# Attention in a three-part kernel: scores of a pair of heads in four steps, transposes in eight, and an order that counts changes of TensorE's tiling

## The chip, the cores and the metric

The kernel runs on one core of a Trainium2 chip. The metric is device time in microseconds (us) of one execution; a lower number is better. Three executions of the kernel before took 2150.86, 2153.95 and 2156.48 us, so the median is 2153.95 us. A further execution was recorded by the hardware profiler; everything read from the trace comes from that one.

## What is computed

Three parts follow each other: an attention with a memory term, a dense mixture of experts (all eight experts on every token, weighted by a normalised table P), and a routed mixture in which a token goes to one expert or to none. The change is in the first part only. Its reference, shortened:

```
B, H, S, D = 4, 8, 576, 64
scores = where(causal, -1e9, q @ k.T / sqrt(D))
a = exp(scores - scores.max(-1));  a /= a.sum(-1)
q_p = where(q > 0, q, exp(q) - 1) + 1
mem_out = (q_p @ M_prev) / (q_p @ z_prev)
g = 1 / (1 + exp(-beta))
out = g * mem_out + (1 - g) * (a @ v)
x = out.transpose(0, 2, 1, 3).reshape(B * S, H * D)      # 2304 x 512, input of the experts
```

All numbers are float32.

## The kernel before

The 32 heads are worked off as 16 pairs. The 576 query rows of a head are cut into five query tiles: tile 0 has 64 rows, tiles 1 to 4 have 128, and because of the causal mask they look at 64, 192, 320, 448 and 576 keys. For a pair the steps are these.

- **scores** (L211, TensorE, matmul on L219): the two heads of a pair have D = 64 each, so head 0 lies on partitions 0 to 63 and head 1 on 64 to 127. Their matmuls use 64 rows of the array each. This is the first of three tilings of the array; the trace shows it as `64*128`. There are six chunks a pair: one for each of the tiles 0 to 3 and two of 288 keys for tile 4. Each chunk takes one PSUM bank per head out of a ring of four banks (two chunks).
- **rowmax** (L224, VectorE): mask, copy into an SBUF tile `pe`, and the row's maximum. There are six `pe` tiles, and ten are needed for a pair.
- **exp** (L239, ScalarE, with the row sums), **mem** (L245, GpSimd: puts the scaled memory query in front of the 64 first columns of `pe`).
- **transposes** (L263, TensorE, L268): blocks of 128 by 128 of `pe` into a PSUM tile `t`, with the whole array, the second tiling (`128*128`). A head has chunks of 1, 2, 3, 4, 4 and 1 blocks; each takes one of two `t` banks. **evac** (L270, ScalarE or VectorE) copies it to SBUF, `pt`.
- **pv** (L285, TensorE, L294): five steps that multiply with the values; the outputs of the two heads lie on 64 columns of the array each, the third tiling (`128*64`).
- **norm** (VectorE) and **norm_rows** (GpSimd, L260) make the row factors; **factors** (L300, TensorE, whole array, L306 and L308, in a `t` bank) turns them, and **finish** (VectorE) multiplies and writes the input `x` of the experts.
- **phi_exp** (ScalarE), **phi** (VectorE), **phi_z** (GpSimd, L199) and **mem_norm** (VectorE) prepare the memory query of a later pair. **logits** (L481, TensorE, 8 columns wide, in a `t` bank) are the gate scores of the experts for the rows of `x` that are done; 13 such steps run inside the attention.

The order of all these steps on each engine is made when the program is built, by a list planner (class `List`, L38). Each step has a length, an urgency, steps that must come before it, and rings of buffers that it takes and gives back. At each moment a free engine takes the ready step with the smallest urgency (L85). The urgency of a step is the pair's number times `PER` plus an entry of the table `AT`. The planner knows nothing of the array's tilings. On the chip each engine then works its list in order, and waits on semaphores where a step isn't ready.

When the last pair is done the experts begin (matmuls on L572); their first weights are requested while the attention still runs.

## Time and profile before

| | us |
|---|---|
| median of three executions | 2153.95 |
| profiled execution, its own time | 2153.33 |
| its span, first to last instruction | 2151.6 |
| attention, from the span's start to the first matmul of the experts | 260.4 |
| TensorE's matmuls busy in the attention | 237.2 |
| VectorE, ScalarE, GpSimd busy in the attention | 171.35, 188.64, 129.50 |
| TensorE busy in the rest, 1891.2 us | 1865.75 |

The busy time of TensorE counts matmuls in flight. The end of a matmul is modelled in the profile, and matmuls overlap; the distance from the start of one group to the start of the next is therefore the better measure of what a group costs. In the trace each float32 matmul of scores and of pv stands as two passes, so a step on two heads reads "x4"; a transpose stands once.

### The profile page before, as it was taken

How to read it: one execution, taken by the hardware profiler on the slowest of the kernel's cores; microseconds unless marked ns; L12 is line 12 of the kernel's file. 1: busy time of each engine (PE TensorE's matmuls, PEld its weight loads, DVE VectorE, ACT ScalarE, POOL GpSimd, SP SyncE). 2: the span in 40 equal slices, each digit the busy share in tenths (PEclk: the TensorE clock that was granted, in tenths of full speed). 3: DMA queues.
4: the chain of work that ended last, by engine and by line, in shares of the span. 5: the costliest groups of instructions: out<-in, count | busy, mean ns of one | idle time of the engine just before them, and what ended most of it. 6: DMA issues, size and time to landing. Idle time of an engine off the chain costs nothing.

```text
span 2151.6 us, 33371 instructions
## 1 busy us (share of the span) xinstructions
PE 2102.9 (98%) x11986; PEld 1771.2 (82%) x11986; DVE 1500.1 (70%) x3182; ACT 804.2 (37%) x1937; POOL 574.6 (27%) x654
## 2 busy tenths in 40 slices
PE   7999899999999999999999999999999999999997
PEld 4455488998899889988888988898899888788886
DVE  5667658777777777777777777777777777434563
ACT  6777632332223223323433322232223223334463
POOL 4445612222222222222312222222222222311121
PEclk9999989999999999999999999999999999899999
DMA  4332211111111111111211211111111111134551
GB/s 113 92 86 74 65 45 40 50 49 41 40 50 50 40 40 50 50 40 55 69 40 49 80 49 40 49 45 45 40 50 50 40 40 64 55 117 150 206 176 50
DMA packets 124800, 138.34 MB, mean 64 GB/s; under 512 B 48202, under 2 KB 83018, under 8 KB 124624
## 3 DMA queue, kind: packets, MB, share of 16 engines
q1 hardware_dynamic: 120704, 126.67, 18.6%
q0 software_dynamic: 3920, 9.44, 1.3%
q8 instruction: 96, 1.57, 0.3%
q14 instruction: 80, 0.66, 0.1%
HBM read 195.86 MB, written 10.75 MB: 96 GB/s over the span
## 4 chain that ended last, share of the span: by engine, by line
PE 89%; DVE 3%; DMA 3%; issue 2%; ACT 1%; POOL 0%; SPq 0%; POOLq 0%; DVEq 0%; ACTq 0%
PE pm L572 32%; PE psy L641 12%; PE psy L643 12%; PE psy L642 12%; PE s L219 3%; PE o L294 3%; PE t L268 3%; DMA out_dram<-o,idx 1%; PE psh L1442 1%; PE psh L1440 1%; PE psh L1441 1%; PE psy L1464 1%; PE psy L1465 1%; PE psy L1466 1%; DMA xg<-out_dram,idx 1%
## 5 line engine op out<-in xcount | busy, mean ns | idle before, releaser
L572 PE MATMUL pm<-xch,w1h 128*128 128x288 f32 (+2 forms) x1792 | 536.5, 299 | 4.2 <-DVE u L585 3.4
L572 PE MATMUL pm<-xch,w1l 128*128 128x288 f32 (+2 forms) x1792 | 531.4, 297 | 2.9 <-DVE w1l L543 2.9
L572 PE MATMUL pm<-xcl,w1h 128*128 128x288 f32 (+2 forms) x1792 | 530.1, 296 | 0.0
L652 DVE SCALAR_TENSOR_TENSOR acc<-psy,pr,acc 128x512 f32<-128x512 f32 x504 | 377.9, 750 | 156.2 <-PE psy L643 145.7
L641 PE MATMUL psy<-w2h,h 128*128 128x512 f32 x1152 | 458.7, 398 | 0.4 <-ACT h L599 0.4
L643 PE MATMUL psy<-w2h,h 128*128 128x512 f32 x1152 | 456.8, 397 | 0.0
L642 PE MATMUL psy<-w2l,h 128*128 128x512 f32 x1152 | 456.3, 396 | 0.0
L585 DVE TENSOR_TENSOR u<-pm,u 128x288 f32<-128x288 f32 (+2 forms) x640 | 290.1, 453 | 121.4 <-PE pm L572 101.3
L572 PEld LDWEIGHTS pm<-xch,w1h 128*128 128x128 f32 x1792 | 339.5, 189 | 10.3 <-DVE u L585 5.9
L572 PEld LDWEIGHTS pm<-xch,w1l 128*128 128x128 f32 x1792 | 339.6, 189 | 3.7 <-DVE w1l L543 3.7
L572 PEld LDWEIGHTS pm<-xcl,w1h 128*128 128x128 f32 x1792 | 339.9, 190 | 2.7
L599 ACT ACTIVATE h<-u 128x288 fp32r<-128x288 f32 (+4 forms) x512 | 182.1, 379 | 361.1 <-DVE u L585 360.9
L537 POOL TENSOR_TENSOR s<-raw 128x256 f32<-128x256 f32 x128 | 95.5, 746 | 819.9 <-issue 800.9
L603 DVE SCALAR_TENSOR_TENSOR h<-u,h 128x288 fp32r<-128x288 f32 (+4 forms) x512 | 258.1, 533 | 69.1 <-ACT h L599 63.1
L609 ACT ACTIVATE u<-pm 128x288 f32<-128x288 f32 (+2 forms) x128 | 51.2, 400 | 682.1 <-PE pm L572 682.1
L643 PEld LDWEIGHTS psy<-w2h,h 128*128 128x128 f32 x1152 | 217.0, 188 | 54.8 <-DVE h L603 1.6
L641 PEld LDWEIGHTS psy<-w2h,h 128*128 128x128 f32 x1152 | 216.8, 188 | 49.5 <-ACT h L599 1.0
L642 PEld LDWEIGHTS psy<-w2l,h 128*128 128x128 f32 x1152 | 216.9, 188 | 49.1
L543 POOL TENSOR_TENSOR w2l<-raw,w2h 128x1024 fp32r<-128x1024 f32 x64 | 154.2, 2410 | 308.5 <-ACT w2h L540 303.6
L268 PEld LDWEIGHTS t<-ident,pe 128*128 128x128 f32 x480 | 54.5, 146 | 64.4 <-issue 25.4
L235 DVE CUSTOM_DVE_ANT_0 pe<-s,mask 128x64 f32<-128x64 f32 (+4 forms) x160 | 65.9, 425 | 49.1 <-PE t L268 38.6
L268 PE MATMUL t<-ident,pe 128*128 128x128 f32 x480 | 85.2, 296 | 12.3 <-ACT pt L283 8.3
(289 smaller groups left out, 2685.9 us busy)
## 6 DMA issues: line engine op xcount, KB each, us to landing
rw<-in_moe_w_dram SPq DMA_DIRECT2D x94, 1024.0 KB
raw<-in_moe_w_dram SPq DMA_DIRECT2D x131, 512.0 KB
qn<-in_qn_dram SPq DMA_DIRECT2D x16, 320.0 KB
vm<-in_vm_dram SPq DMA_DIRECT2D x32, 160.0 KB
q<-in_qT_dram SPq DMA_DIRECT2D x16, 288.0 KB
k<-in_kT_dram SPq DMA_DIRECT2D x16, 288.0 KB
out_dram<-acc SPq DMA_DIRECT2D x18, 256.0 KB
zb<-in_z_prev_dram SPq DMA_DIRECT2D x16, 64.0 KB
```

Source lines behind the costliest of these rows:

```text
L235: nc.vector.tensor_tensor_reduce(s["pe", i][:, 64 + k0:64 + k1], self.raw.pop(("s", n, c)), self.mask[:, m0 + k0:m0 + k1], -0.125, s["nb2" ...
L268: self.nc.tensor.transpose(t[:, kk - k0, :], pe[:, kk * P:(kk + 1) * P], self.ident)
L537: return lambda: nc.gpsimd.tensor_tensor(o, x, y, op)
L543: return lambda: eng.tensor_tensor(o, src, f32(h), ALU.subtract)
L572: nc.tensor.matmul(o, w, x, start=start and k == 0 and i == 0, stop=k == 1 and i == 2, skip_group_check=not start)
L585: nc.vector.tensor_tensor(o, a, b, ALU.add)
L599: nc.scalar.activation(o, src[:, i], AF.Relu)
L603: nc.vector.scalar_tensor_tensor(o, src[:, i], 0.0, f32(hi), ALU.max, ALU.subtract)
L641: nc.tensor.matmul(ps, hh[:, ts], h2[:, f, :], start=f == 0, stop=False)
L642: nc.tensor.matmul(ps, hh[:, ts], l2[:, f, :], start=False, stop=False)
L643: nc.tensor.matmul(ps, hl[:, ts], h2[:, f, :], start=False, stop=f == 1)
L652: nc.vector.scalar_tensor_tensor(a, ps, self.pr[:, j, e:e + 1], a, ALU.mult, ALU.add)
```

## The change

- **Scores in four steps.** `SC` lists for each step the tile, the keys from and to, and the column in the bank. Tiles 1 and 2 (192 + 320 columns) share a bank, tiles 0 and 3 (64 + 448) share one, and tile 4 keeps its two steps of 288. The six pieces of each head stay, and so do the six row maxima.
- **Transposes in eight steps for a pair** in place of twelve: tile 1 of both heads in one bank, tiles 2 and 0 of one head in one bank, the last block of tile 4 of both heads in one bank. The copies out (evac) are as many as before, now up to two from one bank, one after the other.
- **The planner** adds `TURN` to a TensorE step whose tiling differs from the one before it, and `STAY` to its urgency. `PER`, `AT` and the lengths have new values.
- A step that reads a shared bank waits for the whole step that fills it, and a bank comes free when its last reader is done.

The core of the diff:

```
-SC = [(i, k0, k1) for i in range(NQ) for k0, k1 in ([(0, NK[i])] if NK[i] <= 512 else [(0, NK[i] // 2), (NK[i] // 2, NK[i])])]
-TC = [(0, 0, 1), (1, 0, 2), (2, 0, 3), (3, 0, 4), (4, 0, 4), (4, 4, 5)]
+SC = [[(1, 0, 192, 0), (2, 0, 320, 192)], [(0, 0, 64, 0), (3, 0, 448, 64)], [(4, 0, 288, 0)], [(4, 288, 576, 0)]]
+TC = [[(0, 1, 0, 2), (1, 1, 0, 2)], [(0, 2, 0, 3), (0, 0, 0, 1)], [(1, 2, 0, 3), (1, 0, 0, 1)], [(0, 3, 0, 4)], [(1, 3, 0, 4)],
+      [(0, 4, 0, 4)], [(1, 4, 0, 4)], [(0, 4, 4, 5), (1, 4, 4, 5)]]
...
+    TURN, STAY = 0.17, 9.41
...
-                k = min(go, key=lambda k: steps[k][3])
+                turn = {k: e == "PE" and self.mode[k] != mode for k in go}
+                k = min(go, key=lambda k: steps[k][3] + self.STAY * turn[k])
...
-                free[e] = end = now + engines[e]
+                free[e] = end = now + engines[e] + self.TURN * turn[k]
...
-        i, k0, k1 = SC[c]
-        for j in range(2):
-            r = slice(j * 64, j * 64 + 64)
-            o = self.ps_s.tile([P, 512], F32, name="s")[:, :k1 - k0]
-            nc.tensor.matmul(o, q[r, Q0[i]:Q0[i] + P], k[r, k0:k1], start=True, stop=True)
-            self.raw["s", 2 * m + j, c] = o
+        banks = [self.ps_s.tile([P, 512], F32, name="s") for _ in range(2)]
+        for i, k0, k1, a in SC[c]:
+            for j in range(2):
+                r = slice(j * 64, j * 64 + 64)
+                o = banks[j][:, a:a + k1 - k0]
+                nc.tensor.matmul(o, q[r, Q0[i]:Q0[i] + P], k[r, k0:k1], start=True, stop=True)
+                self.raw["s", 2 * m + j, i, k0] = o
...
+    def transposes(self, m, c):
+        t, a = self.ps_t.tile([P, 4, P], F32, name="t"), 0
+        for j, i, k0, k1 in TC[c]:
+            pe = self.st[2 * m + j]["pe", i]
+            self.raw["t", 2 * m + j, i, k0] = t[:, a:a + k1 - k0]
+            for kk in range(k0, k1):
+                self.nc.tensor.transpose(t[:, a, :], pe[:, kk * P:(kk + 1) * P], self.ident)
+                a += 1
...
-    PER = 11.33
+    PER = 12.84
...
```

Three places show what the new order does. The first is TensorE's list in the middle of the attention, before: the transposes of a pair alternate with the next pair's scores (`s` are score banks, `t` transpose banks, `pe` the tiles that are turned; "x4" is four blocks).

```order
L268 MATMUL t_1555<-ident_58,pe_1471 128x128 x4
L219 MATMUL s_1561<-k_1324,q_1323 128x192
L219 MATMUL s_1563<-k_1324,q_1323 128x192
L268 MATMUL t_1578<-ident_58,pe_1490 128x128 x4
L219 MATMUL s_1585<-k_1324,q_1323 128x320
L219 MATMUL s_1587<-k_1324,q_1323 128x320
L268 MATMUL t_1599<-ident_58,pe_1493 128x128 x4
L268 MATMUL t_1605<-ident_58,pe_1490 128x128
L268 MATMUL t_1615<-ident_58,pe_1493 128x128
L219 MATMUL s_1617<-k_1324,q_1323 128x448
L219 MATMUL s_1619<-k_1324,q_1323 128x448
```

The same place after the change:

```order
L229 MATMUL s_1496<-k_1317,q_1316 128x64
L229 MATMUL s_1497<-k_1317,q_1316 128x64
L229 MATMUL s_1496<-k_1317,q_1316 128x448
L229 MATMUL s_1497<-k_1317,q_1316 128x448
L278 MATMUL t_1505<-ident_58,pe_1434 128x128 x4
L278 MATMUL t_1518<-ident_58,pe_1445 128x128 x4
L229 MATMUL s_1540<-k_1317,q_1316 128x288
L229 MATMUL s_1541<-k_1317,q_1316 128x288
L278 MATMUL t_1549<-ident_58,pe_1462 128x128 x4
L278 MATMUL t_1556<-ident_58,pe_1445 128x128
L278 MATMUL t_1556<-ident_58,pe_1462 128x128
```

Two score tiles now stand side by side in one bank, and the two single blocks go to one bank (`t_1556`) where they had a bank each. Over the whole attention TensorE's list changes its tiling 292 times before and 217 times after: into the whole array 128 and 104 times, into the scores' tiling 87 and 49, into that of pv 77 and 64.

The second place is where logits stand on TensorE, in the pair with the most of them, before:

```order
L219 MATMUL s<-k,q 128x64 x2
L268 MATMUL t<-ident,pe 128x128 x4
L219 MATMUL s<-k,q 128x192 x2
L481 MATMUL t<-wg,xA 128x8 x12
L481 MATMUL t<-wg,raw_1878 128x8 x4
L268 MATMUL t<-ident,pe 128x128 x4
L219 MATMUL s<-k,q 128x320 x2
```

After, with the same last logits step (on `raw`, the half-full tile of a batch's end):

```order
L278 MATMUL t<-ident,pe 128x128 x4
L498 MATMUL t<-wg,xA 128x8 x4
L229 MATMUL s<-k,q 128x64 x2
L229 MATMUL s<-k,q 128x448 x2
L498 MATMUL t<-wg,raw_1717 128x8 x4
L278 MATMUL t<-ident,pe 128x128 x8
```

Four logits steps in a row became single ones with scores or transposes between; nowhere in the new list do two logits steps follow each other.

The third place is GpSimd's list at the end of pair 7, where TensorE's factors wait for `rsb` (written by norm_rows), before:

```order
L249 TENSOR_SCALAR pe_1490<-qn_1209,nrm_1331,sums_1368 128x64
L260 TENSOR_TENSOR rsb_1333<-ones_116,rs_1332 128x5x64
L249 TENSOR_SCALAR pe_1493<-qn_1209,nrm_1331,sums_1385 128x64
L260 TENSOR_TENSOR rsb_1333<-ones_116,rs_1332 128x5x64
L199 TENSOR_TENSOR qe_1572<-qn_1417,zb_1418 128x320 x2
```

After:

```order
L258 TENSOR_SCALAR pe_1434<-qn_1181,nrm_1309,sums_1340 128x64
L258 TENSOR_SCALAR pe_1445<-qn_1181,nrm_1309,sums_1327 128x64
L208 TENSOR_TENSOR qe_1465<-qn_1363,zb_1364 128x320 x2
L258 TENSOR_SCALAR pe_1462<-qn_1181,nrm_1309,sums_1340 128x64
L269 TENSOR_TENSOR rsb_1311<-ones_116,rs_1310 128x5x64 x2
```

phi_z (`qe`) now stands ahead of both norm_rows in this pair; before, it stood behind them in seven of the 16 pairs, and after the change it stands ahead of them in all but the first and the last pair.

## Rows read from the trace of the kernel before

**Rows 1.** Windows: busy us (instructions) per engine, granted clock, DMA share, GB/s.

```profile
0.00:260.40 260.40, 237.20 (x1432) 127.42 (x1432) 171.35 (x610) 188.64 (x535) 129.50 (x237) 0.97 0.34 88
260.40:2151.60 1891.20, 1865.75 (x10556) 1643.73 (x10554) 1328.75 (x2572) 615.59 (x1402) 445.12 (x417) 0.99 0.18 61
```

**Rows 2.** Timeline of TensorE around pair 7: start, length, operation, count, idle before.

```profile
122.63 0.65 PE L294 MATMUL o<-pt,vm 128*64 128x256 f32 x4
123.21 0.44 PE L219 MATMUL s<-k,q 64*128 64x64 f32 x4
123.58 0.44 PE L294 MATMUL o<-pt,vm 128*64 128x128 f32 x4
123.95 1.09 PE L268 MATMUL t<-ident,pe 128*128 128x128 f32 x8
124.97 0.60 PE L219 MATMUL s<-k,q 64*128 64x192 f32 x4
125.50 0.65 PE L268 MATMUL t<-ident,pe 128*128 128x128 f32 x4
126.09 0.81 PE L219 MATMUL s<-k,q 64*128 64x320 f32 x4
126.83 0.77 PE L268 MATMUL t<-ident,pe 128*128 128x128 f32 x5
128.17 0.33 PE L268 MATMUL t<-ident,pe 128*128 128x128 f32 x1 [0.58 <-ACT pt L283]
```

**Rows 3.** Timeline of TensorE: two score steps together, and the attention's end.

```profile
240.10 1.65 PE L219 MATMUL s<-k,q 64*128 64x320 f32 x8
241.69 1.09 PE L268 MATMUL t<-ident,pe 128*128 128x128 f32 x8
...
258.10 2.37 PE L294 MATMUL o<-pt,vm 128*64 128x512 f32 x16
260.40 0.40 PE L572 MATMUL pm<-xch,w1h 128*128 128x288 f32 x1
```

**Rows 4.** Groups by shape: count, busy us, mean ns, idle before, its releasers.

```profile
L268 PE MATMUL t<-ident,pe 128*128 128x128 f32 x480 | 85.2, 296 | 12.3 <-ACT pt L283 8.3 <-DVE pt L281 1.7 <-POOL pe L249 1.6
```

**Rows 5.** Windows around two runs of logits, and one without.

```profile
107.20:110.60 3.40, 3.40 (x32) 3.21 (x30) 2.56 (x14) 2.53 (x11) 3.11 (x6) 1.00 0.36 104
110.60:114.00 3.40, 3.40 (x15) 2.21 (x15) 1.20 (x6) 1.51 (x4) 1.84 (x5) 0.50 0.50 118
172.00:178.90 6.90, 6.90 (x26) 4.08 (x26) 3.14 (x8) 2.24 (x5) 2.66 (x6) 0.51 0.24 57
240.00:256.00 16.00, 14.16 (x87) 7.34 (x85) 10.02 (x33) 11.29 (x37) 7.84 (x17) 1.00 0.13 44
```

**Rows 6.** Timeline of TensorE through the second of those runs of logits.

```profile
169.03 2.85 PE L481 MATMUL t<-wg,xA 128*128 128x8 f32 x24
171.74 1.64 PE L481 MATMUL t<-wg,raw 128*128 128x8 f32 x8
173.23 1.09 PE L268 MATMUL t<-ident,pe 128*128 128x128 f32 x4
...
178.46 0.93 PE L268 MATMUL t<-ident,pe 128*128 128x128 f32 x5
```

**Rows 7.** Timelines: the last pair's last scores step, its first long exp.

```profile
248.68 0.76 PE L219 MATMUL s<-k,q 64*128 64x288 f32 x4
...
250.08 0.78 ACT L242 ACTIVATE pe<-pe,nb 128x576 f32<-128x576 f32 x1
250.77 0.19 ACT L242 ACTIVATION_READ_ACCUMULATOR pe<-pe,nb 128x1 f32 x1
```

**Rows 8.** Groups by shape on GpSimd: mem, phi_z, norm_rows.

```profile
L249 POOL TENSOR_SCALAR pe<-qn,nrm,sums 128x64 f32<-128x64 f32 x160 | 66.5, 425 | 101.7 <-ACT pe L242 71.2 <-DVE nrm L209 10.5 <-ACT rb L314 7.6
L199 POOL TENSOR_TENSOR qe<-qn,zb 128x320 f32<-128x320 f32 x32 | 28.0, 897 | 12.7 <-DVE qn L194 12.7
L260 POOL TENSOR_TENSOR rsb<-ones,rs 128x320 f32<-128x320 f32 x32 | 24.0, 757 | 10.5 <-DVE rs L256 10.4
```

More of the change, by code (lines that the diff above doesn't have):

```diff
@@ L71, in run @@
         free, ready = dict.fromkeys(self.ENG, 0.0), {}
-        back, times, now, to_go = [], [0.0], 0.0, len(steps)
+        back, times, now, to_go, mode = [], [0.0], 0.0, len(steps), None
         while to_go:
@@ L347, in run @@
         add, at = li.add, self.AT
-        place = [self.PER * sum(NK[:i]) / sum(NK) for i in range(NQ)]
+        place = [self.PER * x for x in (0, 0.32, 0.64, 0.82)]
         add(("load_beta",), dict(DMA=0.1), self.load_beta, (), at["load"] + 0.2)
@@ new lines, in run @@
+            done = None
+            for c, pieces in enumerate(SC):
+                p = o + place[c] + at["scores"]
+                add(("scores", m, c), dict(PE=self.T_S[c]), self.scores, (m, c), p,
+                    after=[("load", m)] + [("scores", m, c - 1)] * (c > 0), take=dict(s=1), mode="rows",
+                    give=dict(qk=("load", m)) if c == len(SC) - 1 else {})
+                for x, (i, k0, k1, _) in enumerate(pieces):
+                    for j, n in enumerate(heads):
+                        add(("rowmax", n, i, k0), dict(DVE=self.T_MAX[k1 - k0]), self.rowmax, (n, i, k0, k1),
+                            o + place[c] + at["rowmax"] + 0.3 * (2 * x + j),
+                            after=[("scores", m, c), done], take=dict(pe=1) if k0 == 0 else {},
+                            give=dict(s=("scores", m, c)) if j and x == len(pieces) - 1 else {})
+                        done = ("rowmax", n, i, k0)
+                        if k1 == NK[i]:
+                            p = o + place[c] + 0.3 * (2 * x + j)
+                            add(("exp", n, i), dict(ACT=self.T_EXP[i]), self.exp, (n, i), p + at["exp"], after=[done])
+                            add(("mem", n, i), dict(POOL=0.53), self.mem, (n, i), p + at["mem"],
+                                after=[("exp", n, i), ("mem_norm", m)])
@@ new lines, in run @@
+            evacs = []
+            for c, pieces in enumerate(TC):
+                p = o + self.PER * c / len(TC)
+                add(("transposes", m, c), dict(PE=0.11 * sum(k1 - k0 for _, _, k0, k1 in pieces)), self.transposes, (m, c),
+                    p + at["transposes"], after=[("transposes", m, c - 1)] * (c > 0) + [
+                        (s, 2 * m + j, i) for j, i, _, _ in pieces for s in ("exp", "mem")], take=dict(t=1),
+                    give=dict(pe=[("rowmax", 2 * m + j, i, 0) for j, i, k0, k1 in pieces if k1 == i + 1]))
+                for x, (j, i, k0, k1) in enumerate(pieces):
+                    n = heads[j]
+                    add(("evac", n, i, k0), dict(ACT=self.T_EA[k1 - k0], DVE=self.T_ED[k1 - k0]), self.evac, (n, i, k0, k1),
+                        p + at["evac"], after=[("transposes", m, c)] + evacs[:1] + evacs[-1:] * (x > 0), take=dict(pt=1) if c == x == 0 else {},
+                        give=dict(t=("transposes", m, c)) if x == len(pieces) - 1 else {})
+                    evacs.append(("evac", n, i, k0))
@@ L389, in run @@
+            for n in heads:
+                add(("norm", n), dict(DVE=0.54), self.norm, (n,), o + at["norm"], after=[("exp", n, i) for i in range(NQ)] + [("mix",)])
                 add(("norm_rows", n), dict(POOL=0.75), self.norm_rows, (n,), o + at["norm"] + 0.3, after=[("norm", n)])
@@ L391, in run @@
                 add(("pv", m, kk), dict(PE=self.T_PV[kk]), self.pv, (m, kk), o + at["pv"] + kk * 0.5,
[L392 to L393 removed]
+                    after=[("pv", m, kk - 1)] if kk else evacs + [("load_v", n) for n in heads], mode="columns",
+                    take=dict(o=1) if kk == 0 else {}, give=dict(pt=evacs[0]) if kk == NQ - 1 else {})
             p = o + at["factors"]
```

75 lines of the change are left out of this document (22 added, 53 removed).

## Prediction

> **What bounds the kernel now.** I first read the windows by stage. In the attention, 260.4 us long, TensorE's matmuls are busy for 237.2 us, ScalarE for 188.6, VectorE for 171.4 and GpSimd for 129.5; in the rest TensorE is busy for 1865.75 of 1891.2 us [rows 1]. Every stage therefore ends with TensorE. The experts' code is not touched, and their first matmul follows the last pv step without a gap (a pv run starts at 258.10, is 2.37 long, and L572 starts at 260.40) [rows 3]. So what the attention gains or loses should reach the end one to one, and the question is what TensorE's 260 us consist of.
>
> The second view is TensorE's timeline in a stretch where it never waits. The reader is to take the distance from the start of one group to the start of the next, since the lengths overlap [rows 2]. Eight transposes take 124.97 - 123.95 = 1.02 us, and four take 126.09 - 125.50 = 0.59. So one costs (1.02 - 0.59) / 4 = 0.1075, and a group of transposes costs 0.59 - 4 x 0.1075 = 0.16 besides. Scores of 192 columns take 0.53 and of 320 columns 0.74: 0.00164 a column, and 0.215 besides. A pv step of 256 columns takes 0.58 and one of 128 takes 0.37: again 0.00164 a column, and 0.16 besides. Each group with a tiling of its own thus pays 0.16 to 0.215 us that is not work.
>
> Is that the price of a group, or of changing the tiling? Two places tell [rows 3]. The last four pv steps stand together, 512 + 384 + 256 + 128 = 1280 columns: 2.10 us of work by the rate above, 2.30 measured from start to start. They pay 0.20 once, not 4 x 0.16 = 0.64. Scores of 320 and 448 columns back to back take 241.69 - 240.10 = 1.59 for 1.26 of work: 0.33 for two steps, so the second pays about 0.12 in place of 0.215. Eight transposes pay once, by the way they were used above. For transposes and pv the extra cost belongs to the change of tiling; for scores about half of it does.
>
> **The change part by part.** (a) *Fewer changes of tiling.* By the program's order there are 24 fewer entries into the whole array, 13 fewer into pv's tiling and 38 fewer into that of the scores. At the prices above: 24 x 0.16 = 3.8, 13 x 0.16 = 2.1, and 38 x 0.095 (0.215 - 0.12) = 3.6 us at least, 38 x 0.215 = 8.2 at most. That is 9.5 to 14.1 us; I take 10, near the low end, since the pair of score steps in the trace is the nearest row to the new 192 + 320. Nothing hides these, because TensorE is the engine that others wait for. The number of matmuls, row maxima, exps and copies stays.
>
> A rule speaks for less. The Trainium skill (TensorE: Matmul & The Clock Gate, Part 3, The mechanism) says that a weight load overlaps matmuls in flight only when its row group differs. Then a second pv step or a longer run of transposes would still pay its load, and only the drain would be saved; if that is about 0.1 of each 0.16 to 0.215 (an estimate), (a) would be 75 x 0.1 = 7.5. The four pv steps that pay 0.20 together speak against it.
>
> (b) *Banks for the transposes.* Before its transposes TensorE idles for 12.3 us, and 8.3 + 1.7 of them end with a copy out of a `t` bank by ScalarE or VectorE [rows 4]. The typical case is the single block that needs a bank of its own right behind another: 0.58 us idle before a 0.33 us transpose [rows 2]. A pair took 12 banks for its transposes and two for factors; now it takes 8 and two, and the two single blocks share one. That removes between nothing and 10.0 us; I take 7. Against it, a shared bank is copied out in two pieces, one after the other, so it is held longer.
>
> (c) *Logits apart.* TensorE's granted clock in the attention falls to half twice behind a run of logits: 0.50 from 110.6 to 114.0 and 0.51 from 172.0 to 178.9 (1.2 of 2.4 GHz), at 1.00 in the stretch ahead of the first one [rows 5]. The second follows four logits steps in a row [rows 6]. In it, transposes of 4 blocks, scores of 320, transposes of 4 and scores of 448 take 178.46 - 173.23 = 5.23 us; at full clock that is 0.59 + 0.74 + 0.59 + 0.95 (448 x 0.00164 + 0.215) = 2.87. So that dip costs 2.4 in that part and some 0.6 in the logits step at 171.74, which takes 1.49 where the three ahead of it take 0.90 each [rows 6]. That is 3.0 for the second, and half of it, 1.5, for the first, which is half as long. The new order nowhere puts two logits steps together. Between 0 and 4.5 us; I take 4.
>
> (d) *The chain behind the last scores step.* This is where the change can lose. From the last scores step of a pair to its factors the work goes rowmax, exp of two heads (576 columns), mem, norm_rows of two heads. From the rows: scores start to first exp 250.08 - 248.68 = 1.40; two exps 2 x (0.78 + 0.19) = 1.94 [rows 7]; mem 0.43 and two norm_rows 1.51 [rows 8]. With 0.1 us for each of three hand-overs that is 5.6 us. In the new order phi_z, 2 x 0.897 = 1.8 us, stands on GpSimd ahead of norm_rows [rows 8], so the chain is 7.4 where phi_z is ready late. What TensorE has in the meantime in a pair without logits is, at the prices above: last scores step and the next pair's first (288 + 512 columns) 1.31 + 0.215 + 2 x 0.12 = 1.77; transposes of 4 blocks 0.59; scores of 512 columns 0.84 + 0.215 + 0.12 = 1.17; 8 blocks 1.02; scores of 288, 0.69; 6 blocks 0.80. Sum 6.0. Such a pair then waits for between nothing and 7.4 - 6.0 = 1.4 us, and queued behind the waiting factors on TensorE are the pair's five pv steps and everything of the next pair. Other work in ScalarE's queue (phi_exp, copies) can lengthen it by about 1. Ten pairs have no logits in this stretch: 0 to 10 x 2.4 = 24 us. Six have two or three logits steps of 0.9 [rows 6], which cover it. The old order has such waits too, which go: 12.3 less 10.0 in front of the transposes [rows 4] and a little in front of factors. I take a net +6, since half of the pairs by this sum need no wait.
>
> Moved DMAs: the loads of a pair stand in the same sequence on SP but for neighbours exchanged, and the weights of the experts still follow the last of them; at a DMA share of 0.34 [rows 1] I cost that at nothing.
>
> **Sum.** -10 - 7 - 4 + 6 = -15. The profiled execution took 2153.33 us, so 2138.3; the median of the runs shown is 0.6 higher, so I say **2139**.
>
> **The rivals.** *The chain takes the place of the switches* (slower). Place: factors and the first pv step, behind norm_rows on GpSimd and phi_z in front of them. Price: 2.4 us in every pair that has a phi_z there, 14 x 2.4 = 34, less (a), (b) and (c), 21: 2153.3 + 13 = 2166. It decides from 21 / 14 = 1.5 us a pair on. For it: GpSimd's new order, and the exps' place behind phi_exp. Against: six pairs have logits there. Between this and the forecast lies the case that new waits eat just the gain, about 2152.
>
> *The long runs of transposes take the clock down* (slower). Price of a dip like the shorter one, 1.5 us, in each of 16 pairs: 24, so 2163. Against it: from 240 to 256, with eight transposes in a row at 241.69, the clock is 1.00 [rows 3, 5]. The Trainium skill (TensorE: Matmul & The Clock Gate, Part 4: PE-mode transpose) says that transposes don't count as busy in the way that matmuls do, and the new order has up to ten in a row; that rule would give the 2163, and the stretch at 240 doesn't bear it out.
>
> *The change does not do what it says*: half of what I call switching stays with the group, and the banks bring nothing. Then -5 - 0 - 4 + 6 = -3, 2151.
>
> *All of it works and no new wait comes*: -14 - 10 - 4.5 = -28.5, 2125.
>
> **How the numbers follow.** The forecast's own band, 2131 to 2147, has 0.57; the full gain, below 2131, 0.17; gains eaten by waits or not there (2147.5 to 2160), 0.17; slower by the chain 0.07; by the clock 0.02. A measurement of this kernel tells about 0.3%, 6.5 us, from no change, so faster means below 2147.5 and slower above 2160.4: 0.74, 0.17 and 0.09. The range reaches from 2126 (near the full gain) to 2152 (gains just eaten); about 0.1 lies on either side.
>
> **What would show it.** If (a) is right, pv steps in a row stand at distances of columns x 0.00164 with one extra of 0.16 to 0.2, and the attention's matmuls are busy for less than 237 us. If (b) is right, the idle time in front of transposes that ends with a copy out of `t` falls from 10.0 to 3 or so, and no single block waits 0.58. If (c) is right, the granted clock stays 1.00 from 30 to 250 us. If (d) is worse than I think, idle time appears in front of factors and of the 64-column pv step, ending with rsb from GpSimd or with a late copy from ScalarE, in the pairs without logits. The first matmul of the experts should start near 245 us, and the rest should keep its 1891 us; if the rest differs by more than 3 us (its first microseconds stand right behind the attention, and a clock dip there can be longer or shorter), the forecast fails for a reason outside the change. It would also be wrong if the attention's new bound were ScalarE, whose 188.6 us leave room today.

## The result, and the profile after

The changed kernel took 2130.83 us (median of four executions, 2130.08 to 2133.57) beside 2153.95 before; the ratio is 0.9896 with a 95% interval of 0.9879 to 0.9913. It gains 23 us where 15 were forecast (2139, range 2126 to 2152). The profiled execution took 2130.76 us, with a span of 2128.9.

The windows of the changed kernel, cut at the first matmul of the experts (columns as in [rows 1]):

```profile
0.00:238.73 238.73, 218.08 (x1433) 124.81 (x1433) 163.99 (x600) 189.85 (x545) 132.11 (x237) 1.00 0.38 96
238.73:2128.90 1890.17, 1866.19 (x10556) 1643.71 (x10554) 1329.90 (x2572) 616.16 (x1402) 445.24 (x417) 0.99 0.19 61
```

The attention ends 21.7 us earlier than in [rows 1], the rest is 1.0 shorter. TensorE's matmuls are busy for 218 us of it and were for 237, with the same matmuls; ScalarE is busy for 189 us before and 190 after, and comes closer to being the bound. The granted clock of the attention is 1.00, where it was 0.97.

TensorE's timeline of the changed kernel at three places (start, length, operation, count):

```profile
20.87 1.25 PE L229 MATMUL s<-k,q 64*128 64x64 f32 x8
22.05 1.09 PE L278 MATMUL t<-ident,pe 128*128 128x128 f32 x8
...
101.07 1.62 PE L229 MATMUL s<-k,q 64*128 64x288 f32 x12
102.62 0.66 PE L278 MATMUL t<-ident,pe 128*128 128x128 f32 x4
...
236.42 2.38 PE L304 MATMUL o<-pt,vm 128*64 128x512 f32 x16
238.73 0.40 PE L589 MATMUL pm<-xch,w1h 128*128 128x288 f32 x1
```

Twelve score matmuls in a row are 288 + 192 + 320 = 800 columns on both heads. From start to start they take 1.55 us; at 0.00164 a column the work is 1.31, so three pieces pay 0.24 once, about what one step alone paid in [rows 2]. The trace has twelve such runs of three pieces; eight pay 0.24, and four pay 0.55, because one head's part waits for its bank there. 64 + 448 columns take 22.05 - 20.87 = 1.18 for 0.84 of work, 0.34: there the second piece pays some 0.12. The last four pv steps take 2.31 for 2.10, as in [rows 3].

The groups of transposes, of factors and of the 288-column scores in the changed kernel (busy us, mean ns, idle before, releasers):

```profile
L278 PE MATMUL t<-ident,pe 128*128 128x128 f32 x480 | 77.6, 287 | 7.8 <-POOL pe L258 5.0 <-DVE pt L291 1.6 <-ACT pt L293 0.7
L316 PE MATMUL t<-ident,rsb 128*128 128x128 f32 x64 | 10.3, 283 | 3.5 <-ACT pt L293 1.7 <-DVE nb L244 1.6
L229 PE MATMUL s<-k,q 64*128 64x288 f32 x128 | 28.8, 463 | 1.0 <-DVE nb L244 1.0
```

The row of the factors before, not shown so far:

```profile
L306 PE MATMUL t<-ident,rsb 128*128 128x128 f32 x64 | 10.3, 284 | 2.4 <-ACT pt L283 2.3
```

Beside [rows 4]: idle time that ends with a copy out of a `t` bank fell from 10.0 to 2.3 us. Idle time that ends with `pe` from GpSimd, which is mem (L258), rose from 1.6 to 5.0, and that before factors from 2.4 to 3.5. The factors' waits are waits for a `t` bank as well: 1.7 us end with ScalarE's copy, and where the row names `nb` (52.20, 121.58 and 209.46 in the timeline), VectorE's copy of a full `t` bank had ended 0.15 us earlier each time.

Some of these waits in TensorE's timeline of the changed kernel (idle before and releaser in brackets):

```profile
118.39 0.75 PE L229 MATMUL s<-k,q 64*128 64x288 f32 x2
119.36 0.75 PE L229 MATMUL s<-k,q 64*128 64x288 f32 x2 [0.23 <-DVE nb L244]
...
121.58 0.63 PE L316 MATMUL t<-ident,rsb 128*128 128x128 f32 x4 [0.66 <-DVE nb L244]
...
175.98 1.10 PE L278 MATMUL t<-ident,pe 128*128 128x128 f32 x8 [0.72 <-POOL pe L258]
...
229.76 1.06 PE L278 MATMUL t<-ident,pe 128*128 128x128 f32 x8
231.81 0.66 PE L278 MATMUL t<-ident,pe 128*128 128x128 f32 x4 [0.99 <-POOL pe L258]
233.05 0.87 PE L278 MATMUL t<-ident,pe 128*128 128x128 f32 x6 [0.58 <-POOL pe L258]
```

The largest stand at the last pair, where no scores of a next pair are left to fill the time. The row lists none of the matmuls' idle time before factors as ending with `rsb` (norm_rows). The weight loads of the factors do wait for `rsb`, 6.4 us at nine places (1.8 at two before), but mostly while earlier matmuls are still in flight. At two places (94.30 and 150.73) the factors start 0.06 us behind the end of norm_rows and 0.4 us behind the transpose ahead of them in place of 0.11, which makes 0.6 us in all.

The first two lines show a wait that counts only in part as idle time. The matmuls of one head run at 118.39 while the other head's bank is still full. The next transposes start at 120.05, so the step takes 1.66 us where a 288-column step takes 0.69; only 0.23 of the difference is idle.

Windows of the changed kernel at the times of the half-clock stretches of [rows 5], at the start, and at the experts' first matmuls (the last three columns are granted clock, DMA share, GB/s):

```profile
15.00:21.80 6.80, 5.67 (x36) 3.42 (x36) 4.84 (x25) 5.05 (x14) 3.95 (x9) 1.00 0.28 87
172.00:178.90 6.90, 5.93 (x44) 3.51 (x46) 5.76 (x23) 6.56 (x20) 5.83 (x7) 1.00 0.69 185
243.10:260.20 17.10, 16.10 (x70) 15.75 (x70) 8.41 (x14) 5.54 (x12) 7.39 (x6) 0.50 0.10 31
```

No stretch of the attention is at half clock any more. The one behind the attention, 17.1 us long, stands in both kernels (in the kernel before it starts at 264.2).

**The account.** From the first scores to the experts' first matmul it was 260.40 - 7.52 = 252.88 us before and is 238.73 - 7.97 = 230.76 after: -22.1. The rows give -4.5 for idle time before transposes (12.3 to 7.8), +1.1 before factors, and +0.5 before scores (0.8 to 1.3, without the first load). Two experiments below price the half-clock stretches: -3.9 for the two behind logits, -2.5 for the one at the start. What is left, 22.1 - 4.5 - 3.9 - 2.5 + 1.6 = 12.8 us, is put down to the 75 changes of tiling: 0.17 each. This last is a remainder; it lies in the 9.5 to 14.1 that the rows gave beforehand.

The two traces also allow a direct estimate. It takes every group of one tiling at the extra that such a group pays where nothing waits: 0.17 us for pv, 0.16 for transposes, and for scores 0.215 for a step alone (0.26 for 64 columns), 0.24 for 288 + 192 + 320 and 0.34 for 64 + 448. That makes 53.0 us before and 40.1 after, so 12.9 less: 7.0 in the scores, 3.8 in the transposes, 2.2 in pv. What this count leaves over is about 2 us more of waiting that isn't idle time, as at 118.39, and some 8 us in place of 6.4 for the half-clock stretches. So the items are good to about 2 us, and no run took the fewer changes alone.

### The profile page after: what moved, and what is told of

It is laid out like the page before. It is cut to its first block, busy times and chain, and to the rows that moved or that the text cites. A ratio compares the mean times of both kernels' runs of the same rounds, so it can differ in the third digit from the quotient of the medians.

```text
span 2128.9 us, 33313 instructions
## 1 busy us (share of the span) xinstructions
PE 2084.3 (98%) x11986; PEld 1768.5 (83%) x11986; DVE 1493.9 (70%) x3172; ACT 806.0 (38%) x1947; POOL 577.4 (27%) x654
## 4 chain that ended last, share of the span: by engine, by line
PE 88%; DVE 4%; issue 4%; POOL 2%; DMA 1%; ACT 1%; POOLq 0%; SPq 0%; DVEq 0%; ACTq 0%
PE pm L589 32%; PE psy L658 13%; PE psy L659 12%; PE psy L660 12%; PE o L304 2%; PE psh L1459 2%; PE psh L1457 2%; PE psh L1458 2%; PE t L278 2%; PE psy L1481 2%; PE psy L1482 2%; PE psy L1483 2%; PE pst L1435 1%; PE s L229 1%; POOL pe L258 1%
## 5 line engine op out<-in xcount | busy, mean ns | idle before, releaser
L258 POOL TENSOR_SCALAR pe<-qn,nrm,sums 128x64 f32<-128x64 f32 x160 | 71.8, 460 | 95.9 <-ACT pe L251 73.5
L244 DVE CUSTOM_DVE_ANT_0 pe<-s,mask 128x192 f32<-128x192 f32 (+4 forms) x160 | 65.5, 421 | 39.2 <-PE t L278 33.3
```

The source lines that it names most:

```text
L258: nc.gpsimd.tensor_scalar(s["pe", i][:, 0:64], qn[:, j, i, :], nrm[:, j, i:i + 1], s["sums"][:, i:i + 1], ALU.mult, ALU.mult)
```

## The experiments

All are complete kernels, and the planner makes each list anew. The tables of urgencies belong to the order that they were written for, so an undone part can cost a misfit besides its own price. The ratios are to the kernel before, on the same chip. "Changes" are changes of tiling in TensorE's list of the attention; "at half" is the time between first scores and first experts' matmul in which the profiled execution had a granted clock of half, from the records of the clock in the trace; "attention" is from one to the other. These last two columns come from one execution of each kernel, which can lie some us from the median (2162.24 in e_before_apart, 2154.20 in e_before_wide, 2153.40 in e_tc12, 2148.08 in e_logits_run, 2147.39 in e_run_wide). On the chips of the experiments the kernel before had medians of 2152.65 to 2154.35, so medians of different kernels compare to about 2 us.

| kernel | median us | ratio, 95% | changes | attention us | at half us |
|---|---|---|---|---|---|
| before | 2153.95 | 1 | 292 | 252.9 | 17.1 |
| changed | 2130.83 | 0.9896 (0.9879 to 0.9913) | 217 | 230.8 | 0 |
| e_stay0 | 2165.02 | 1.0052 (1.0032 to 1.0071) | 246 | 260.1 | 27.3 |
| e_tc12 | 2157.61 | 1.0021 (1.0011 to 1.0032) | 249 | 252.4 | 13.7 |
| e_sc6_tc12 | 2192.27 | 1.0181 (1.0156 to 1.0207) | 230 | 291.1 | 68.3 |
| e_before_stay | 2164.98 | 1.0045 (1.0028 to 1.0062) | 244 | 266.1 | 51.2 |
| e_phiz | 2129.82 | 0.9896 (0.9878 to 0.9914) | 213 | 229.8 | 0 |
| e_before_apart | 2154.46 | 1.0013 (0.9993 to 1.0034) | 291 | 256.2 | 23.9 |
| e_logits_run | 2154.15 | 1.0003 (0.9992 to 1.0014) | 212 | 252.3 | 34.1 |
| e_before_wide | 2148.88 | 0.9977 (0.9964 to 0.9990) | 292 | 249.0 | 6.8 |
| e_run_wide | 2152.88 | 1.0009 (0.9999 to 1.0019) | 212 | 249.3 | 17.1 |
| e_tc12_wide | 2157.89 | 1.0027 (1.0017 to 1.0037) | 249 | 258.5 | 23.9 |
| e_after_wide | 2133.96 | 0.9922 (0.9903 to 0.9941) | 217 | 236.3 | 10.2 |
| e_start_wide | 2133.22 | 0.9905 (0.9889 to 0.9922) | 217 | 233.2 | 6.8 |

The theory after the result: the gain is fewer changes of tiling, banks, and clock, and the half-clock stretches come from runs of logits. The rival: any place where TensorE waits or is thinly used may bring them, so every added wait is paid twice.

### The parts undone one by one

**e_stay0**: the planner counts changes, but doesn't hold a step back for them.

```
-    TURN, STAY = 0.17, 9.41
+    TURN, STAY = 0.17, 0.0
```

> The kernel after with STAY = 0: shared banks, tables and TURN as after, but the planner no longer prefers to stay in a tiling. 246 changes of tiling in place of 217. If a change costs 0.16 to 0.2 us: 29 of them, +5 to +6, near 2136. If only the banks matter, 2131.

It took 2165.02 us, 34 more than the changed kernel and 11 more than before. Two groups of TensorE's in e_stay0:

```profile
L229 PE MATMUL s<-k,q 64*128 64x288 f32 x128 | 32.7, 477 | 7.9 <-DVE nb L244 7.2
...
L316 PE MATMUL t<-ident,rsb 128*128 128x128 f32 x64 | 11.3, 305 | 7.1 <-ACT pt L293 4.5 <-POOL pe L258 1.1 <-DVE pt L291 0.8
```

A window of e_stay0 (granted clock third from the end):

```profile
180.80:191.00 10.20, 8.96 (x30) 4.08 (x29) 4.70 (x16) 5.09 (x14) 8.05 (x12) 0.50 0.16 39
```

29 more changes at 0.17 make 5.0 us of the 29.4 that its attention is longer. Idle time before the 288-column scores goes from 1.0 in the changed kernel to 7.9 (they wait for a row maximum to free a bank), before factors from 3.5 to 7.1, before transposes from 7.8 to 9.0: 11.7. That leaves 12.7, and 27.3 us stand at half clock. So the parts are not additive: the new tables without the new rule run scores into full banks.

**e_tc12**: transposes in twelve steps, each in a bank of its own.

```
-TC = [[(0, 1, 0, 2), (1, 1, 0, 2)], [(0, 2, 0, 3), (0, 0, 0, 1)], [(1, 2, 0, 3), (1, 0, 0, 1)], [(0, 3, 0, 4)], [(1, 3, 0, 4)],
-      [(0, 4, 0, 4)], [(1, 4, 0, 4)], [(0, 4, 4, 5), (1, 4, 4, 5)]]
+TC = [[(0, 1, 0, 2)], [(1, 1, 0, 2)], [(0, 2, 0, 3)], [(0, 0, 0, 1)], [(1, 2, 0, 3)], [(1, 0, 0, 1)], [(0, 3, 0, 4)], [(1, 3, 0, 4)],
+      [(0, 4, 0, 4)], [(1, 4, 0, 4)], [(0, 4, 4, 5)], [(1, 4, 4, 5)]]
```

> The kernel after with twelve transposes steps a pair, each with a bank of its own, as before; everything else as after. The order has 249 changes of tiling in place of 217. By the price of a change 32 x 0.16 to 0.2 = 5 to 6.5 us come back; if the waits for single blocks' banks were worth about 7, they come back too: 2136 from the first alone, 2143 with both.

2157.61 us, 27 more than the changed kernel. The group of transposes in e_tc12:

```profile
L278 PE MATMUL t<-ident,pe 128*128 128x128 f32 x480 | 89.0, 293 | 20.7 <-POOL pe L258 9.7 <-DVE pt L291 5.0 <-ACT pt L293 4.9
```

TensorE's timeline in e_tc12 where a half-clock stretch begins, and the window of the stretch:

```profile
178.33 0.76 PE L278 MATMUL t<-ident,pe 128*128 128x128 f32 x5 [1.64 <-POOL pe L258]
179.67 0.47 PE L278 MATMUL t<-ident,pe 128*128 128x128 f32 x1 [0.58 <-ACT pt L293]
...
179.20:182.60 3.40, 2.93 (x14) 1.86 (x16) 0.40 (x5) 2.56 (x10) 3.40 (x4) 0.50 0.49 116
```

Waits that end with a copy out of a bank are 9.9 us here and 2.3 in the changed kernel: the shared banks are worth 7.6 us of waiting before transposes in the new order, near the 7.7 of step (b), and the single block that waits 0.58 is back. The 32 more changes are 5.4 us at 0.17. Most of the rest of the added idle time is mem, 5.0 to 9.7. Behind the waits for mem (0.76 us at 175.19, 1.64 at 178.33), with no logits in the 8 us ahead, the granted clock goes to half (179.2, for 3.4 us).

**e_sc6_tc12**: transposes in twelve steps, scores in six as well, with places and lengths of the six steps entered in the tables; the planner's rule stays.

```
-SC = [[(1, 0, 192, 0), (2, 0, 320, 192)], [(0, 0, 64, 0), (3, 0, 448, 64)], [(4, 0, 288, 0)], [(4, 288, 576, 0)]]
+SC = [[(1, 0, 192, 0)], [(2, 0, 320, 0)], [(0, 0, 64, 0)], [(3, 0, 448, 0)], [(4, 0, 288, 0)], [(4, 288, 576, 0)]]
...
```

> The kernel after with no shared banks at all: six scores steps and twelve transposes steps a pair as before, but the planner's TURN and STAY and the tables of after. 230 changes of tiling. If the order makes most of the gain and the banks a third of it: 13 more changes, +2.5, and bank waits +7: 2140. If the banks are needed for all of it, near 2150; if they bring nothing, 2133.

2192.27 us, the slowest of all, with only 230 changes. Its group of transposes:

```profile
L278 PE MATMUL t<-ident,pe 128*128 128x128 f32 x480 | 94.7, 314 | 23.7 <-POOL pe L258 10.7 <-ACT pt L293 8.4 <-DVE pt L291 3.4
```

62 changes fewer than before, and 38 us slower: the number of changes alone doesn't tell the time. Its attention stands at half clock for 68 us. Six score steps with the shared transposes banks were not run, so the score banks' own part isn't separated.

**e_before_stay**: the kernel before with the planner's rule alone, old banks and old tables.

```
-                k = min(go, key=lambda k: steps[k][3])
+                turn = {k: e == "PE" and MODE(k) != mode for k in go}
+                k = min(go, key=lambda k: steps[k][3] + self.STAY * turn[k])
...
-                free[e] = end = now + engines[e]
+                free[e] = end = now + engines[e] + self.TURN * turn[k]
...
```

> The kernel before with one part of the change alone: its planner adds TURN (0.17) to a TensorE step with another tiling and STAY (9.41) to its urgency. Steps, banks and tables are those of before. The order has 244 changes of tiling in place of 292, and one run of three logits steps. If a change of tiling costs 0.16 to 0.2 us, 48 fewer give -8 to -10, and with one of the two clock dips gone about -2 more: near 2144. If the shared banks made the gain, this stays at 2154 or is slower by new waits.

48 changes fewer, which at 0.17 are 8 us, and 11 us slower. TensorE's timeline in e_before_stay shows a wait of a new kind:

```profile
172.57 0.59 PE L227 MATMUL s<-k,q 64*128 64x64 f32 x4 [2.06 <-DMA k<-in_kT_dram]
```

The window of e_before_stay behind it:

```profile
172.70:182.90 10.20, 8.90 (x33) 4.48 (x34) 5.89 (x20) 5.19 (x14) 8.31 (x9) 0.50 0.16 39
```

Scores kept together ask for the next keys 2.06 us before they are there, and the clock falls behind that wait (a single logits step stands at 168.2, and a run of two at 197.8 ahead of another stretch at 200.0). With the old banks and the old tables the rule loses; which of the two it lacks was not run apart.

### The chain behind the last scores step

**e_phiz**: the changed kernel with a later urgency for phi_z, meant to bring it behind norm_rows on GpSimd.

```
-    AT = dict(load=-1.14, load_v=12.32, pair=-5.15, phi=-63.82, phi2=-4.35, phi_z=-56.65, mem_norm=-0.15, scores=-6.74, rowmax=-4.77,
+    AT = dict(load=-1.14, load_v=12.32, pair=-5.15, phi=-63.82, phi2=-4.35, phi_z=4.0, mem_norm=-0.15, scores=-6.74, rowmax=-4.77,
```

> The kernel after with the urgency of phi_z set so late that GpSimd does both norm_rows of a pair ahead of the next pair's phi_z; 213 changes of tiling. If the waits in front of factors (about 5 us in all in the trace of after) come from phi_z standing ahead of norm_rows, they go: 2126. If phi_z is then late for mem of the next pair, waits move in front of the transposes: 2131 or more.

2129.82 us; its ratio can't be told from that of the changed kernel. (The rows of the changed kernel give 3.5 us before factors, not the 5 named beforehand.) The group of transposes in e_phiz, and GpSimd's timeline in one of its pairs:

```profile
L278 PE MATMUL t<-ident,pe 128*128 128x128 f32 x480 | 77.1, 285 | 7.4 <-POOL pe L258 5.5 <-ACT pt L293 0.7 <-DVE pt L291 0.7
...
89.70 1.68 POOL L208 TENSOR_TENSOR qe<-qn,zb 128x320 f32<-128x320 f32 x2
91.34 1.41 POOL L269 TENSOR_TENSOR rsb<-ones,rs 128x320 f32<-128x320 f32 x2
```

The edit did not move phi_z: it (`qe`) still stands ahead of both norm_rows (`rsb`) in 14 pairs, and GpSimd's order of phi_z, mem and norm_rows differs from the changed kernel's only up to the first pair's norm_rows. So the equal waits (3.5 us before factors in both, 5.5 and 5.0 for mem) say nothing of phi_z, and no run here puts it behind norm_rows.

The trace of the changed kernel says something instead. Of the eleven waits for mem before transposes, two (17.19 and 162.04, 0.57 of 5.0 us) end with a mem that stood directly behind phi_z on GpSimd, and one (233.05, 0.58) with a mem behind norm_rows; ahead of the mem that ends the other eight, GpSimd had itself been waiting, mostly for an exp. Most of the waiting for mem thus comes from the exps, not from phi_z.

### The clock

**e_before_apart**: the kernel before with its logits steps pulled apart, so that at most two follow each other.

```
-                    j, u = p * NTP + c, last * at.PER + at.AT["logits"]
+                    j, u = p * NTP + c, last * at.PER + at.AT["logits"] + 3.2 * (c % 4)
```

> The kernel before with the urgencies of the logits steps set 3.2 apart, so that no more than two stand in a row (before: up to four); 291 changes of tiling, as before. If runs of logits bring the granted clock down, the stretches at half clock behind 110 and 172 us vanish and the time falls by 3 to 4.5 us, to 2150. If the clock falls for another reason, they stay and the time is 2154.

2154.46 us, no gain. Its profiled execution lies 8 us above its median; it has 10.2 us at half clock from 109.7, behind a run of two logits steps, and a stretch at 236.0 without logits. Moving them also moved other steps: idle time before transposes is 15.7 us where it was 12.3. The experiment doesn't separate the two theories, since it changes waits and logits together.

**e_logits_run**: the changed kernel with its logits in runs of 4, 5 and 4 steps.

```
-                    add(("logits", j), dict(PE=0.9), lambda j=j: out.update({j: m1.logits(j)}), (), u,
-                        after=[dep], take=dict(t=1))
...
+        for last, js in group.items():
+            add(("logits", last), dict(PE=0.9 * len(js)), lambda js=js: [m1.logits(j)() for j, _ in js], (),
+                last * at.PER + at.AT["logits"], after=[dep for _, dep in js], take=dict(t=2), give=dict(t=("logits", last)))
```

> The kernel after with the 13 logits steps put into three runs of four, five and four; 212 changes of tiling (after: 217). If runs of logits bring the clock down, stretches at half clock come back behind the runs, 1.5 to 3 us each, so 2130.8 - 1 + 4.5 to 9: near 2136. If not, 2130 and a granted clock of 1.00 throughout the attention.

2154.15 us: the whole gain is gone. TensorE's timeline in e_logits_run at the first run:

```profile
77.89 1.06 PE L498 MATMUL t<-wg,xA 128*128 128x8 f32 x8 [0.25 <-ACT pt L293]
79.20 2.85 PE L498 MATMUL t<-wg,xA 128*128 128x8 f32 x24 [0.26 <-DVE pr L499]
```

The window of e_logits_run behind it:

```profile
82.70:89.50 6.80, 5.95 (x25) 3.15 (x23) 2.86 (x14) 3.64 (x12) 2.77 (x8) 0.50 0.01 2
```

A half-clock stretch stands behind each of the three runs. But a run also holds both `t` banks, so waits come with it, and this doesn't yet tell the 8-column matmuls from the waits. The next four kernels do: they leave every list as it is and make only the logits' matmuls 128 columns wide, by reading the eight gate columns 16 times.

```
-            nc.tensor.matmul(ps, x[:, k, :P], self.wg[:, k, :], start=k == 0, stop=k == KT - 1)
+            w = self.wg[:, k, :]
+            if self.WIDE:
+                w = w.unsqueeze(1).to_broadcast([P, P // E, E])
+            nc.tensor.matmul(ps, x[:, k, :P], w, start=k == 0, stop=k == KT - 1)
...
```

**e_before_wide**: the kernel before with that edit.

> The kernel before with the same edit: logits 128 columns wide, in the old order with four logits steps in a row. Theory narrow (it is the narrow matmuls of a run of logits that take the granted clock to half): the stretches at 110.6 (3.4 us) and 172.0 (6.8 us) go, the one at 15.0, which has no logits near, stays; 1.5 + 3.0 us less, so about 2149.5. Theory waiting (TensorE's idle time around them does it, whatever the width): both stretches stay and the time is 2154.

2148.88 us, a ratio of 0.9977 (0.9964 to 0.9990) and so some 5 us less, between 2 and 8, near the 4.5 expected. The timeline of e_before_wide through the second run of logits:

```profile
168.54 2.95 PE L484 MATMUL t<-wg,xA 128*128 128x128 f32 x24
171.32 1.10 PE L484 MATMUL t<-wg,raw 128*128 128x128 f32 x8
```

Its windows, the first at the start, the other two at the times of the stretches in [rows 5]:

```profile
16.10:22.90 6.80, 6.80 (x29) 4.41 (x29) 4.60 (x21) 3.90 (x12) 3.64 (x8) 0.50 0.30 95
110.60:114.00 3.40, 3.40 (x26) 2.26 (x24) 2.35 (x10) 1.74 (x6) 2.88 (x6) 1.00 0.49 115
172.00:178.90 6.90, 6.32 (x40) 3.65 (x41) 5.17 (x15) 4.64 (x13) 3.92 (x6) 1.00 0.24 57
```

A step on 128 columns takes 2.78 / 3 = 0.93 us, one on 8 took 0.90 [rows 6]: width costs next to nothing. Both stretches behind logits are gone, the one at the start stays, and the attention is 256.95 - 7.99 = 248.96 us, 3.9 shorter. Both signs, the two stretches and the median, say that in the list of before the 8-column runs took the clock down; the profile is a single one. Its execution took 2154.20 us all the same, the slowest of twelve, because the part behind the attention took 1895.5 us where before took 1891.2, with more of it at half clock.

**e_run_wide**: e_logits_run with that edit.

> The changed kernel with its logits in runs of 4, 5 and 4 steps, as before, but 128 columns wide. With 8 columns that order took 2154.15, with stretches at half clock behind each of the three runs (82.7, 157.8, 209.0, together 23.8 us) and two at 14.5 and 253.4 that have no logits near. Theory narrow: the three stretches go, and about half of their length with them: 2154 - 12 = 2142. Theory waiting: nothing moves, 2154, since the runs' waits stay (0.25 us twice ahead of each).

2152.88 us; the ratios to before, 1.0009 and 1.0003, don't differ, so the 12 us of the narrow theory did not come. The windows of e_run_wide behind the three runs:

```profile
82.70:89.50 6.80, 5.32 (x35) 2.60 (x35) 3.76 (x18) 3.87 (x13) 3.07 (x8) 1.00 0.00 0
...
161.10:164.50 3.40, 3.40 (x12) 0.96 (x12) 1.96 (x5) 2.91 (x11) 1.82 (x4) 0.50 0.00 0
208.90:215.70 6.80, 5.61 (x21) 3.02 (x23) 3.47 (x11) 3.98 (x14) 4.26 (x7) 0.50 0.01 2
```

Its timeline ahead of the last of these:

```profile
206.61 0.75 PE L229 MATMUL s<-k,q 64*128 64x288 f32 x2 [1.11 <-DVE nb L244]
207.29 1.09 PE L278 MATMUL t<-ident,pe 128*128 128x128 f32 x8
209.19 1.54 PE L278 MATMUL t<-ident,pe 128*128 128x128 f32 x6 [0.81 <-DVE pt L291]
```

The first stretch is gone, the second went from 10.2 to 3.4 us, and the third stays: behind that run TensorE waits 1.11 and 0.81 us. Both theories hold here, each at its place. Of the time between first scores and the experts, TensorE's matmuls are busy for 234.07 us in e_logits_run and 227.97 in e_run_wide, and idle for 18.3 and 21.4 (12.7 in the changed kernel). So the width took 6.1 us off and new waits gave 3.1 back. Of the 18.6 us that e_run_wide's attention is longer than the changed kernel's, 8.7 are idle time.

**e_tc12_wide**: e_tc12 with that edit.

> The changed kernel with twelve transposes steps in banks of their own, and logits 128 columns wide. With 8 columns that order took 2157.61, with stretches at half clock at 15.4, 179.2 and 254.3 (13.6 us in all); the two later ones stand behind pieces in which TensorE waited 2.3 and 2.0 us for mem on GpSimd, with no logits in the 8 us ahead. Both theories: the width changes nothing here, the stretches stay, 2157. If they go too, the stretches hang on something that neither theory has.

2157.89 us, as without it. The window of the first of the two stretches behind waits for mem:

```profile
185.70:189.10 3.40, 3.40 (x16) 1.84 (x17) 0.23 (x2) 2.68 (x8) 3.40 (x4) 0.50 0.37 86
```

Both stay at the same steps (now at 185.7 and 260.8). Two more stand at 42.3 and 168.6, where e_tc12 has none. So narrow logits are not needed for a half-clock stretch; that the waits bring these is the likeliest reading, but no run took the waits away alone.

**e_after_wide**: the changed kernel with that edit.

> The changed kernel with one edit: the gate logits' matmuls are 128 columns wide in place of 8 (the eight gate columns read 16 times, seven eighths and more of the result unused; same steps in the same order). It prices the width itself. An 8-column matmul stands 0.112 us from the next in the traces so far, 128 columns by 0.00164 us a column for two passes make 0.105 a pass, so a logits step should keep its 0.90 us. The order has no stretch at half clock in the attention to lose. Both theories: 2131, within 2 us of the changed kernel.

2133.96 us, a little above the expected band, with executions from 2131.79 to 2145.43. Its profiled execution has half-clock stretches at 17.8 and 55.4 that the changed kernel's doesn't have, though the width can't reach either of them (the first logits stand at 78.6). The stretch behind the attention, on the other hand, is short in it:

```profile
253.40:256.80 3.40, 3.40 (x17) 3.40 (x16) 1.10 (x4) 1.49 (x3) 1.40 (x4) 0.50 0.11 42
```

**e_start_wide**: the changed kernel with its attention untouched; only the logits among the experts' first matmuls are 128 wide.

> The changed kernel with its attention untouched, and only the gate logits that stand among the experts' first matmuls made 128 columns wide. In the changed kernel the granted clock is half from 243.1 to 260.2 there; it begins behind waits of 1.24, 0.46 and 0.73 us for weights, and four logits steps of 8 columns stand in it (246.9, 251.5, 254.6, 259.2) between matmuls that follow each other without a gap. Theory narrow: these steps keep the clock down, the stretch shrinks to 7 to 10 us and some 4 us go, 2127. Theory waiting: only the waits ahead of it count, 17 us as before and 2131. The attention up to 238.7 is the same program as in the changed kernel, so it also asks whether the start without a half-clock stretch comes again: if 7 us at half clock stand near 15 to 18 us, as in the same order with wide logits, that start is a matter of tenths of a microsecond, and 2 to 4 us of the gain with it.

2133.22 us, not the 2127 of the narrow theory. Three windows of e_start_wide:

```profile
15.80:22.60 6.80, 6.18 (x29) 4.17 (x29) 4.60 (x21) 3.77 (x10) 2.85 (x8) 0.50 0.26 87
244.50:251.30 6.80, 5.75 (x23) 5.40 (x24) 4.07 (x6) 1.90 (x5) 5.20 (x5) 0.50 0.23 77
...
1029.60:1039.80 10.20, 10.20 (x45) 9.71 (x44) 4.24 (x9) 3.54 (x7) 7.09 (x6) 0.50 0.38 130
```

The stretch behind the attention shrank from 17.1 to 6.8 us, as that theory said. This does not show that the width did it: in e_after_wide, whose logits among the experts are still 8 wide, it is 3.4 us. And two others came where the program is the same as the changed kernel's: at the start, and 10.2 us in the middle of the experts. The first answers the question that was put to this run. TensorE's timeline at the start in the changed kernel:

```profile
15.06 1.29 PE L229 MATMUL s<-k,q 64*128 64x288 f32 x4 [0.51 <-DVE nb L244]
16.29 0.55 PE L278 MATMUL t<-ident,pe 128*128 128x128 f32 x3
17.19 0.77 PE L278 MATMUL t<-ident,pe 128*128 128x128 f32 x5 [0.35 <-POOL pe L258]
```

The same steps in e_start_wide:

```profile
14.14 1.29 PE L229 MATMUL s<-k,q 64*128 64x288 f32 x4 [0.78 <-DVE nb L244]
15.37 0.55 PE L278 MATMUL t<-ident,pe 128*128 128x128 f32 x3
16.28 1.33 PE L278 MATMUL t<-ident,pe 128*128 128x128 f32 x5 [0.36 <-POOL pe L258]
```

The distances are the same to 0.01 us, and all of it stands 0.91 to 0.92 earlier; then five transposes take 0.77 in one and 1.33 in the other. This attention takes 233.24 us where the changed kernel's took 230.76, with the same 12.7 us of idle time, so the stretch costs 2.5. The list doesn't decide whether it comes; when the work falls is what differs between the two, and is the likely reason.

## Why the prediction was right

Faster, in the range, and by the three savings it named; the place of the new waits was wrong, and the gain is 8 us larger than its sum. Some 2.5 us of that are luck: a half-clock stretch at the start that the changed kernel's profile happens to lack. By its steps:

- **(a) fewer changes, taken -10, remainder -12.8, counted -12.9.** The mis-sized term was the scores, taken at 3.6 to 8.2 and near the low end, counted at 7.0. The one pair of score steps in the trace of before (320 and 448) paid 0.12 for the second, and I took that for all; in the changed kernel 192 + 320 behind a 288 pay next to nothing more where no bank is waited for, and only 64 + 448 pays about 0.12. The upper bound, 14.1, was the nearer one. The Trainium skill (TensorE: Matmul & The Clock Gate, Part 3, The mechanism) lets a weight load overlap matmuls in flight only where the row group differs. The 0.24 for twelve score matmuls on the same two row groups speaks against it. The 7.5 us of the prediction's rival rest on 0.1 us a change, which no run shows; 12.8 over 75 changes is 0.17.
- **(b) banks, taken -7, measured -7.7** in the rows before transposes, and 7.6 by e_tc12. Right, and the 0.58 before single blocks is gone. Against it, some 1 us more of waiting for a bank stands before factors (2.3 to 3.3); whether a shared bank that is held longer brings it wasn't tested.
- **(c) clock, taken -4, measured -3.9** by e_before_wide for the two stretches that it spoke of. Right for the list of before. As a general reason it was too narrow: half-clock stretches stand behind waits without logits as well (e_tc12, e_tc12_wide). The stretch at the start, worth 2.5 us, wasn't counted: the prediction looked for half clock behind logits only, and its sign on the clock began at 30 us.
- **(d) new waits, taken +6, measured +5.0** (mem +3.4, factors +1.1, scores +0.5). The size is near, the place was wrong. I put it before factors, behind norm_rows and phi_z; there idle time rose by 1.1, which belongs to the banks, and the row lists none of it as ending with `rsb`. Only the 0.6 us at 94.30 and 150.73 are of the forecast kind. Most of the new waits are a step earlier in the same chain: exp, mem, then the transposes. phi_z stands directly ahead of the mem in only 0.57 of those 5.0 us; its place was not tested by a run, since e_phiz left it where it was. The chain does end late, but it should have been followed to its first reader on TensorE, not to its last. The waits of scores in which one head's bank is full were not in the sum at all.
- **The rest** kept its 1891 us within 1.0, so the attention's gain reached the end one to one.

The rivals: the chain as a bound didn't come, since the waits are in other places and shorter than 1 us. Transposes in runs didn't take the clock down: the granted clock is 1.00 over the attention's 238.73 us, with eight in a row at 22.05 and at 175.98, and with nothing but 18 transposes and four turns of factors from 229.76 to 235.04. The Trainium skill (TensorE: Matmul & The Clock Gate, Part 4: PE-mode transpose) states that transposes don't count as busy in the way that matmuls do. This trace doesn't bear that out. "It does not do what it says" is excluded by TensorE's 218 us.

What the forecast couldn't have told from its reasons is how near the loss lay. Each of three edits that undo a part or the order of the logits loses all the gain: 34, 27 and 23 us (e_stay0, e_tc12, e_logits_run), where changes and banks by themselves would be 5, 13 and next to nothing. What comes on top are waits of a misfit list, and half-clock stretches behind them. How much of it is the one and how much the other isn't settled exactly; at 0.37 to 0.54 us for each us at half clock (2.5 for 6.8 in e_start_wide, 3.9 for 10.2 in e_before_wide, 5.5 for 10.2 in e_after_wide, with 0.4 of added idle time in it), the 34 us at half in e_logits_run are 13 to 18 of its 21.6, and 5.6 are added idle time.

## What to carry to other kernels

Price a change of the array's tiling from distances between group starts, with a place in the trace where steps of one tiling stand together: here it was 0.17 us. It was saved only where buffers were merged and the order was set along with it; keeping a tiling with the old banks and tables ran into late loads and lost 11 us. Follow a chain that gets tighter to its first reader on the bounding engine. Count the granted clock as a cost that may come with waiting: e_stay0 added 5 us of changes and 11.7 of waits, and lost 29, with 27.3 us at half clock. Where very narrow matmuls must run in a row, widening them can be nearly free.

## What was not expected of the hardware

- **Width at almost no cost.** Runs of 8-column matmuls are followed by half clock in the list of before (0.50 and 0.51), and the same runs 128 columns wide are not (1.00 and 1.00), at 0.93 us a step beside 0.90.
- **The same program, other stretches.** The same list with the same distances ahead of the stretch had 6.8 us at half clock near 16 us or none, and 10.2 us of it near 1030 or none (changed kernel and e_start_wide). The Trainium skill (TensorE: Matmul & The Clock Gate, Part 1, What's actually happening) says that the number of slow matmuls at a kernel's start varies from run to run. The traces agree for the start, and show it in the middle of the experts as well. A profile's stretch is therefore worth its 2 to 5 us only if a second profile, or an edit that leaves the order alone, has it too. Executions of the kernel before on one chip ranged from 2147.47 to 2156.44 us.
